# Attention and a gated feed-forward on one core: every bfloat16 product of TensorE given as two of 64 weight columns

## The chip, the core and the metric

The kernel runs on one core of a Trainium2 chip. A core has TensorE (matrix products; PE in the profile, with its weight loads as PEld), VectorE (DVE), ScalarE (ACT), GpSimd (POOL) and SyncE (SP, which here only issues transfers). Products are written to PSUM, which has eight banks; everything else lives in SBUF, and transfers to and from the chip's memory are run by 16 DMA engines. The metric is the device time of one execution in microseconds, less is better.

## The reference

For 8 batches of 8 heads with 576 positions of 64 values each, causal attention with a forgetting gate, and then a gated feed-forward layer on all 4,608 tokens:

```python
scores = scale * np.matmul(q, k.transpose(0, 1, 3, 2))
log_f = np.log(np.clip(f, 0.0001, 1.0))
cum = np.cumsum(log_f, axis=-1)
decay = cum[:, :, :, None] - cum[:, :, None, :]
scores = np.where(causal, -1000000000.0, scores + decay)
attn = softmax(scores)                       # max taken off, exp, divided by the sum
attn_out = np.matmul(attn, v)
x = attn_out.transpose(0, 2, 1, 3).reshape(B * S, H * D)      # 4608 x 512
g = x @ w_gate                                                # 512 x 1536
silu = g * (1.0 / (1.0 + np.exp(-g)))
out = (silu * (x @ w_val)) @ w_out                            # 1536 x 512
```

Inputs and the result are float32; the kernel computes its products in bfloat16 and sums them in float32.

## The kernel before

Two heads form a pair, `p`, of which there are 32, four in each batch. The 128 rows of a tile are 64 query rows of one head and the same 64 of the other. Each head's 576 positions are nine blocks of 64 (`i`), in two groups: `g` = 0 holds blocks 0 to 3 and `g` = 1 blocks 4 to 8.

On TensorE, a head pair goes through these steps:

- Transposes of q and k (L467; L546 for the first four pairs). The inputs lie with positions on the partitions; products with the identity turn them, six of 96 columns for k and eight of 72 for q. The result goes to PSUM (`tx`) and is copied to `kt` and `qz`. `qz` holds each head's query block in its own half of the partitions, with zeros in the other, so that one product of 128 rows serves both heads.
- Scores (L594) and mask (L598). For each block `i` the weights are `qz[:, i]`, 128 columns, and the moving operand is the pair's keys up to the block's end, 64 to 512 columns at a time. On the diagonal block a second product, of the identity with a mask of 64 columns, adds the causal mask. The table `BANKS` says which products share a PSUM bank (`sp`).
- VectorE adds the decay and takes the row minimum (L622), ScalarE takes the exponential (L642), GpSimd divides by the sum into `pk` (L678).
- The attention weights are transposed from `pk` to `pT`: for the first eight pairs on TensorE (L708, 128 columns each, 25 of them per pair), for the others by a DMA.
- Output (L734): for every chunk `c` of 128 key positions, two products, one for each head: 64 weight columns of `vt` and that head's columns of `pT`, written to PSUM partitions 0 to 63 and 64 to 127. So this product alone is already given as two halves of 64 weight columns. For `g` = 1 the five chunks have 320, 320, 320, 192 and 64 columns, for `g` = 0 the two chunks 256 and 128; from the ninth pair on the two groups are one operation of 14 products.
- `spread` copies the result to `xT` (L758), where it lies as the feed-forward needs it.

The feed-forward works on tiles of tokens, `TILES` = 256, 256, seven times 512, 256, 128, 128. `gate` (L816) multiplies `wg` and `wv`, as weights of 128 x 128, with `xT`, four products into each 128 rows of the hidden layer; tanh, two VectorE products and a rounding to bfloat16 follow (`th`, `hh`). `project` (L844) takes `hh` as weights and 512 columns of `wo` as the moving operand, twelve products for each 128 tokens, and the result goes out through `ot`.

The order of all instructions is set before launch: `Plan.order` is a list scheduler with a cost for each operation and engine, priorities, and the tiles' buffers; its result is written out as it stands. The costs given for TensorE's operations (`mm`, and the sums beside the transposes) are numbers in the source and do not follow from what is issued. Ahead of the first scores, `select` (L395) spreads the decay by a float32 product; it is not touched.

Of the kernel before, what the change touches and what calls it, by code (L numbers as in the profile page):

```python
# [32 lines left out]
class Plan:  # L33
# [29 lines left out]
    def order(self):  # L63
# [126 lines left out]
        assert len(done) == len(self.ops), [o.writes for o in self.ops if o.start is None][:10]  # L190
        self.span = max(o.end for o in done)
        return sorted(done, key=lambda o: (o.start, o.n))


def mm(*cols):
# [4 lines left out]
def kernel(  # L200
# [234 lines left out]
    def prepare(p):  # L435
        s = first[p]
        if p < NHALF:
            prepare_parts(p)
            return
        for name in ("k", "q"):  # L440
            fk, bk = (name + "f", p), (name + "b", p)
            KR, KC = ROWS[name]
            pl.key(bk, name + "b")

            def cast(e, name=name, fk=fk, bk=bk, KR=KR):
                src = pl.buf(fk)[0:KR, :, :].rearrange("p h (r d) -> p r h d", d=D)
                dst = pl.buf(bk)[0:KR, :, :, :]
                if e == "ACT":
                    nc.scalar.activation(dst, src, AF.Copy, scale=-scale if name == "q" else 1.0)
                elif name == "q":  # L450
                    eng[e].tensor_scalar(dst, src, -scale, 1.0, op0=ALU.mult, op1=ALU.mult)  # L451
                else:
                    eng[e].tensor_copy(dst, src)
            engs = {"POOL": 850 if p < 8 else 800 if name == "k" else 1010}
            if p < NPB:
                engs = {"POOL": 850, "ACT": 850, "DVE": 500} if name == "k" else {"POOL": 1050, "ACT": 1050, "DVE": 680}
            o = pl.op(engs, cast, [fk], [bk], s - 1 + (name == "q") * .1)
            o.bias = SPARE if p else {}
            tk = ("tt", name, p)
            pl.key(tk, "tx", line="q")  # L460
            ok = ("kt", p) if name == "k" else ("qz", p)
            pl.key(ok, ok[0])

            def transpose(e, bk=bk, tk=tk, KR=KR, KC=KC):
                src = pl.buf(bk).rearrange("p r h d -> p r (h d)")
                for j in range(KC):
                    nc.tensor.transpose(half(tk)[:, KR * j:KR * j + KR], src[0:KR, j, :], ident[0:KR, 0:KR])  # L467
            pl.op({"PE": KC * (KR / 2.4 + 2.5)}, transpose, [bk], [tk, ok], s - 1, lat=200)
            halves = [(0, P, None)] if name == "k" else [(0, 64, 0), (64, 128, 1)]
            for a, z, h in halves:  # L470
                def evac(e, a=a, z=z, h=h, tk=tk, ok=ok, KC=KC):
                    if h is None:
                        src = half(tk)[a:z, 0:S].rearrange("r (j p) -> r p j", j=KC)
                        dst = pl.buf(ok)[a:z, :].rearrange("r (p j) -> r p j", j=KC)
                    else:
                        src = half(tk)[a:z, 0:S].rearrange("r (j i p) -> r i p j", j=KC, i=NB)
                        dst = pl.buf(ok)[a:z, :, h, :].rearrange("r i (p j) -> r i p j", j=KC)
                    if e == "ACT":
                        nc.scalar.copy(dst, src)
                    else:  # L480
                        nc.vector.tensor_copy(dst, src)  # L481
                o = pl.op({"ACT": 600, "DVE": 680}, evac, [tk] + ([("z", "qz", p)] if h is not None and p < len(pl.pools["qz"]) else []), [ok, (ok, "done")], s - .9)
                o.bias = LATER if p >= 8 else {}
# [34 lines left out]
    def prepare_parts(p):  # L518
        for name, x, a, z, r, n in parts(p):
# [23 lines left out]
            def transpose(e, bk=bk, tk=tk, r=r, w=m * n):  # L543
                src = pl.buf(bk).rearrange("p r h d -> p r (h d)")
                for j in range(r):
                    nc.tensor.transpose(half(tk)[:, w * j:w * j + w], src[0:w, j, :], ident[0:w, 0:w])  # L546
            pl.op({"PE": r * (m * n / 2.4 + 2.5)}, transpose, [bk], [tk] + (oks if x == "A" else []), pr, lat=200, holds=oks)
            for u in range(n):
                for lo, hi, h in ([(0, P, None)] if name == "k" else [(0, 64, 0), (64, 128, 1)]):
# [31 lines left out]
    def scores(p, g):  # L581
# [3 lines left out]
        for n, bank in enumerate(BANKS[g]):  # L585
# [4 lines left out]
            def mult(e, bank=bank, sk=sk):  # L590
                sp, kt, qz, o = pl.buf(sk), pl.buf(("kt", p)), pl.buf(("qz", p)), 0
                for i, a, z in bank:
                    last = z == QB * (i + 1)
                    nc.tensor.matmul(sp[:, o:o + z - a], qz[:, i, :, :].rearrange("p h r -> p (h r)"), kt[:, a:z],  # L594
                                     start=True, stop=not last or p >= MFROM)
                    o += z - a
                    if last and p < MFROM:
                        nc.tensor.matmul(sp[:, o - QB:o], ident, mask, start=False, stop=True)  # L598
            cols = [z - a for _, a, z in bank] + [64 for i, a, z in bank if z == QB * (i + 1) and p < MFROM]
            pl.op({"PE": mm(*cols)}, mult, pair_done(p, g) + ["mask"], [sk], pr, lat=220, holds=[("kt", p), ("qz", p)])  # L600
            o = 0
# [46 lines left out]
    def normalize(p, g):  # L648
# [51 lines left out]
        for a in range(0, NSL[g], 8):  # L700
            z = min(a + 8, NSL[g])
            bk = ("tt", p, g, a)
            pl.key(bk, "gv", line="p")
            bank = lambda bk=bk: half(bk)

            def transpose(e, a=a, z=z, bank=bank):
                for x in range(a, z):
                    nc.tensor.transpose(bank()[:, P * (x - a):P * (x - a) + P], pl.buf(kk)[:, x, :], ident)  # L708
            pl.op({"PE": 56 * (z - a)}, transpose, [kk], [bk], s, lat=300)

            def evac(e, a=a, z=z, bank=bank):
                dst = pl.buf(tk)[:, a:z, :].rearrange("p s k -> p (s k)")
                (nc.scalar.copy if e == "ACT" else nc.vector.tensor_copy)(dst, bank()[:, :P * (z - a)])  # L713
            pl.op({"DVE": 64 * (z - a) / .96 + 90, "ACT": P * (z - a) * .833 + 110}, evac, [bk], [tk], s)
# [86 lines left out]
    def gate(t, tok, n):  # L801
        nf = 512 // n
        x0 = tok % NRING
        assert x0 + n <= NRING
        for u in range(KF // nf):
            fcs = range(u * nf, u * nf + nf)
            xs = [("x", hp, m) for hp in range(KD) for m in range(tok // QB, (tok + n) // QB)]
            pr = 1000 + t * 20 + u
            for nm, wt in (("wg", wg), ("wv", wv)):
                bk = (nm, t, u)  # L810
                pl.key(bk, "gv", line="f")

                def mult(e, wt=wt, bk=bk, fcs=fcs):
                    for j, fc in enumerate(fcs):
                        for ko in range(KD):
                            nc.tensor.matmul(pl.buf(bk)[:, j * n:j * n + n], wt[:, ko, fc * P:fc * P + P],  # L816
                                             xT[:, ko, x0:x0 + n], start=ko == 0, stop=ko == KD - 1)
                o = pl.op({"PE": mm(*[n] * (KD * nf))}, mult, xs + [(nm, fc) for fc in fcs], [bk], pr, lat=220)
                gates_of[t] = o
            pl.key(("th", t, u), "th")  # L820
            pl.key(("hh", t, u), "hh")
            pl.op({"ACT": 487}, lambda e, u=u: nc.scalar.activation(pl.buf(("th", t, u)), pl.buf(("wg", t, u)), AF.Tanh, scale=0.5),  # L822
                  [("wg", t, u)], [("th", t, u)], pr - 5000, lat=120)
            pl.op({"DVE": 605}, lambda e, u=u: nc.vector.scalar_tensor_tensor(  # L824
                pl.buf(("th", t, u)), pl.buf(("th", t, u)), 1.0, pl.buf(("wg", t, u)), op0=ALU.add, op1=ALU.mult),
                [("th", t, u), ("wg", t, u)], [("u", t, u)], pr - 5000, lat=180)
            pl.op({"DVE": 605}, lambda e, u=u: nc.vector.tensor_mul(pl.buf(("hh", t, u)), pl.buf(("th", t, u)), pl.buf(("wv", t, u))),  # L827
                  [("u", t, u), ("th", t, u), ("wv", t, u)], [("hh", t, u)], pr - 5000, lat=100)

    def project(t, tok, n):  # L830
        nf = 512 // n
        for ms in range(n // P):
# [4 lines left out]
            for a, z in ((0, DM // 2), (DM // 2, DM)) if end else ((0, DM),):  # L837
                bk = ("op", t, ms, a)
                pl.key(bk, "gv", line="o")
                for f0 in range(0, KF, 4):  # L840
                    def mult(e, f0=f0, ms=ms, bk=bk, a=a, z=z):
                        for fc in range(f0, f0 + 4):
                            hh = pl.buf(("hh", t, fc // nf))
                            nc.tensor.matmul(pl.buf(bk)[:, 0:z - a], hh[:, (fc % nf) * n + ms * P:(fc % nf) * n + ms * P + P], wo[:, fc, a:z],  # L844
                                             start=fc == 0, stop=fc == KF - 1)
                    pl.op({"PE": mm(*[z - a] * 4)}, mult, [("hh", t, fc // nf) for fc in range(f0, f0 + 4)] +
                          [("wo", fc) for fc in range(f0, f0 + 4)] + ([(bk, f0)] if f0 else []), [bk, (bk, f0 + 4)], pr, lat=220)

# [123 lines left out]
```

## Time and profile before

| what | value |
|---|---|
| median of 3 runs | 419.02 us (418.44 to 419.73) |
| profiled execution: span | 417.2 us |
| PE busy | 398.3 us, 95% |
| DVE / ACT / POOL busy | 79% / 74% / 60% |
| TensorE instructions in the program | 6,579 |

The page gives no time of the profiled execution other than its span, from the first to the last instruction; the median of the runs lies 1.8 us above it. In the profile, a row of the timeline gives the start in us, the time from the first start to the last end, the engine, the source line, the operation, the tiles, and the shape: `128*64` means 128 rows of the array and 64 weight columns, and `128x320` means 320 columns streamed. The end of a matmul is modelled and reaches into the next, so what a product costs in a stream is read from start to start. A table of stretches gives for each engine its busy us and, in brackets, the number of its instructions in the stretch.

### The profile page before, as it was taken

To read this page: it belongs to the slowest core of one execution; us is meant where nothing else is said; L and a number is where in the kernel's file an instruction comes from. 1 tells how busy PE (TensorE), PEld (TensorE's weight loads), DVE (VectorE), ACT (ScalarE), POOL (GpSimd) and SP (SyncE) were. 2 spreads that over 40 slices of the span, in tenths; PEclk is the share of its full clock that TensorE was granted. 3 is DMA by queue.
4 is the path that set the end of the run, shared out by engine and by line. 5 is a ranking of instruction groups with operands and counts; after the bars stand their busy time and mean duration, and the time that the engine had idled before them with its cause. 6 is when DMAs were issued, how large, how long until landed. Compare 5 with 4: busy or idle time off the path is not lost.

```text
span 417.2 us, 9955 instructions
## 1 busy us (share of the span) xinstructions
PE 398.3 (95%) x3250; PEld 232.3 (56%) x3296; DVE 328.9 (79%) x1065; ACT 310.3 (74%) x872; POOL 251.7 (60%) x459
## 2 busy tenths in 40 slices
PE   1979999999999999999999999999999999999996
PEld 0636878665555555555555554555555444457675
DVE  5688999999998899989897797798967764565232
ACT  4798999989995999899999984798996533232221
POOL 7589698987887897976968678267773400000000
PEclk9998999999999999999999999999999999999999
DMA  9999979695999999899999999848999211000211
GB/s 183 253 210 225 190 135 252 159 234 141 200 229 215 264 218 236 203 232 222 228 234 218 240 221 223 194 116 190 221 217 186 55 37 50 25 27 25 77 52 52
DMA packets 144004, 71.83 MB, mean 172 GB/s; under 512 B 117904, under 2 KB 131728, under 8 KB 143952
## 3 DMA queue, kind: packets, MB, share of 16 engines
q1 hardware_dynamic: 137568, 65.95, 71.1%
q0 software_dynamic: 5808, 4.72, 7.6%
q10 hardware_dynamic: 576, 0.52, 0.5%
q8 instruction: 26, 0.43, 0.4%
q14 instruction: 26, 0.21, 0.3%
HBM read 46.65 MB, written 9.58 MB: 135 GB/s over the span
## 4 chain that ended last, share of the span: by engine, by line
PE 86%; DVE 4%; issue 1%; ACT 0%
PE gv L816 43%; PE gv L844 22%; PE sp L594 9%; PE tx L734 6%; PE tx L467 3%; PE sp L598 2%; PE gv L708 2%; DVE t L622 1%; DVE pT L713 1%; DVE hh L827 1%; DVE th L824 1%; DVE qz L481 1%; DVE kt L481 0%; ACT ot L851 0%; DVE tm L622 0%
## 5 line engine op out<-in xcount | busy, mean ns | idle before, releaser
L622 DVE CUSTOM_DVE_ANT_0 t<-sp,cb 128x320 f32<-128x320 f32 (+7 forms) x288 | 130.4, 475 | 12.1 <-PE sp L598 8.6
L678 POOL TENSOR_SCALAR pk<-e,lr 128x128 bf16<-128x128 f32 (+3 forms) x190 | 100.5, 533 | 61.8 <-DVE lr L660 16.5
L816 PE MATMUL gv<-xT,wg 128*128 128x512 bf16 (+2 forms) x563 | 110.6, 327 | 0.8
L816 PE MATMUL gv<-xT,wv 128*128 128x512 bf16 (+2 forms) x562 | 109.3, 324 | 0.9
L844 PE MATMUL gv<-wo,hh 128*128 128x512 bf16 (+1 forms) x425 | 104.2, 373 | 0.8
L824 DVE SCALAR_TENSOR_TENSOR th<-th,gv 128x512 f32<-128x512 f32 x108 | 73.9, 684 | 39.3 <-ACT th L822 38.3
L822 ACT ACTIVATE th<-gv 128x512 f32<-128x512 f32 x108 | 64.1, 594 | 44.0 <-PE gv L816 43.1
L642 ACT ACTIVATE e<-t,tm 128x576 f32<-128x576 f32 (+4 forms) x160 | 88.7, 556 | 8.9 <-DVE tm L622 8.3
L827 DVE TENSOR_TENSOR hh<-th,gv 128x512 bf16<-128x512 f32 x108 | 73.7, 685 | 8.7 <-PE gv L816 4.9
L642 ACT ACTIVATE eo<-t,tm 128x128 f32<-128x128 f32 (+3 forms) x128 | 71.1, 556 | 4.7 <-DVE tm L622 2.9
L594 PE MATMUL sp<-kt,qz 128*128 128x448 bf16 (+6 forms) x320 | 71.9, 293 | 1.5 <-DVE tm L622 1.4
L678 POOL TENSOR_SCALAR pk<-eo,lr 128x128 bf16<-128x128 f32 (+3 forms) x127 | 67.6, 532 | 5.4 <-DVE lr L660 3.1
L816 PEld LDWEIGHTS <-wg 128*128 128x128 bf16 x576 | 49.8, 98 | 35.7
L816 PEld LDWEIGHTS <-wv 128*128 128x128 bf16 x576 | 48.9, 98 | 33.7 <-issue 0.3
L844 PEld LDWEIGHTS <-hh 128*128 128x128 bf16 x444 | 39.9, 98 | 39.0
L598 PE MATMUL sp<-mask,ident 128*128 128x64 bf16 x288 | 48.0, 197 | 0.0
L594 PEld LDWEIGHTS <-qz 128*128 128x128 bf16 x320 | 30.9, 100 | 20.9 <-DVE tm L622 0.9
L851 ACT ACTIVATE ot<-gv 128x512 f32<-128x512 f32 (+1 forms) x31 | 17.9, 580 | 27.1 <-PE gv L844 26.2
L598 PEld LDWEIGHTS <-ident 128*128 128x128 bf16 x288 | 27.2, 100 | 12.6 <-issue 1.9
L734 PE MATMUL tx<-pT,vt 128*64 128x320 bf16 (+4 forms) x448 | 29.6, 266 | 1.9 <-DVE pT L713 1.3
L451 POOL TENSOR_SCALAR qb<-qf 72x1024 bf16<-72x1024 f32 x28 | 29.1, 1041 | 3.1 <-DMA qf<-in_q_dram 2.0
L642 ACT ACTIVATION_READ_ACCUMULATOR e<-t,tm 128x1 f32 x160 | 30.6, 192 | 0.0
(69 smaller groups left out, 389.0 us busy)
## 6 DMA issues: line engine op xcount, KB each, us to landing
out_dram<-ot SPq DMA_DIRECT2D x35, 256.0 KB
vf<-in_v_dram SPq DMA_DIRECT2D x32, 256.0 KB
cb<-cum_f SPq DMA_DIRECT2D x56, 144.0 KB
kf<-in_k_dram SPq DMA_DIRECT2D x28, 288.0 KB
qf<-in_q_dram SPq DMA_DIRECT2D x28, 288.0 KB
wo<-in_moe_w_out_dram POOLq DMA_DIRECT2D x3, 512.0 KB, 10.8
vf<-in_v_dram SPq DMA_DIRECT2D x8, 128.0 KB
wv<-in_moe_w_val_dram POOLq DMA_DIRECT2D x2, 512.0 KB, 8.4
```

The costliest lines, as they stand in the source:

```text
L451: eng[e].tensor_scalar(dst, src, -scale, 1.0, op0=ALU.mult, op1=ALU.mult)
L594: nc.tensor.matmul(sp[:, o:o + z - a], qz[:, i, :, :].rearrange("p h r -> p (h r)"), kt[:, a:z], start=True, stop=not last or p >= MFROM)
L598: nc.tensor.matmul(sp[:, o - QB:o], ident, mask, start=False, stop=True)
L622: nc.vector.tensor_tensor_reduce(out=pl.buf(tk)[:, a:z], in0=pl.buf(sk)[:, o:o + z - a], in1=pl.buf(("cm", p))[:, i, :] if own else pl.buf ...
L642: nc.scalar.activation(pl.buf(ek)[:, :L], pl.buf(tk)[:, :L], AF.Exp, bias=pl.buf(("tm", p, g))[:, 0, i:i + 1], scale=-1.0, accum_out=pl.bu ...
L678: eng[e].tensor_scalar(dst, src, r, 1.0, op0=ALU.mult, op1=ALU.mult)
L734: nc.tensor.matmul(xo[r, 0:QB * n], vt[:, c, 2 * hp + h, :], pT[:, a:a + n, 64 * h:64 * h + 64], start=(c == 0), stop=(c == nch - 1))
L816: nc.tensor.matmul(pl.buf(bk)[:, j * n:j * n + n], wt[:, ko, fc * P:fc * P + P], xT[:, ko, x0:x0 + n], start=ko == 0, stop=ko == KD - 1)
L822: pl.op({"ACT": 487}, lambda e, u=u: nc.scalar.activation(pl.buf(("th", t, u)), pl.buf(("wg", t, u)), AF.Tanh, scale=0.5), [("wg", t, u)], ...
L824: pl.op({"DVE": 605}, lambda e, u=u: nc.vector.scalar_tensor_tensor(pl.buf(("th", t, u)), pl.buf(("th", t, u)), 1.0, pl.buf(("wg", t, u)), ...
L827: pl.op({"DVE": 605}, lambda e, u=u: nc.vector.tensor_mul(pl.buf(("hh", t, u)), pl.buf(("th", t, u)), pl.buf(("wv", t, u))), [("u", t, u), ...
L844: nc.tensor.matmul(pl.buf(bk)[:, 0:z - a], hh[:, (fc % nf) * n + ms * P:(fc % nf) * n + ms * P + P], wo[:, fc, a:z], start=fc == 0, stop=f ...
```

## The change

Two helpers are added. `columns` gives a product as two: the first uses weight columns 0 to 63 and writes partitions 0 to 63 of the output, the second uses columns 64 to 127 and writes partitions 64 to 127; both stream the same moving operand and carry the same start and stop marks. `turned` does so for transposes. Every bfloat16 product and transpose but L734 goes through them; L734 has this form already and L395 is float32. The planner's costs are as they were, and the order of operations is kept. Each of these products now takes two weight loads and two matmuls.

```diff
+def columns(nc, out, lhsT, rhs, **kw):
+    for h in range(2):
+        c = slice(64 * h, 64 * h + 64)
+        nc.tensor.matmul(out[c, :], lhsT[:, c], rhs, **kw)
+
+
+def turned(nc, out, src, ident):
+    for h in range(2):
+        c = slice(64 * h, 64 * h + 64)
+        nc.tensor.transpose(out[c, :], src[:, c], ident)
...
-                    nc.tensor.transpose(half(tk)[:, KR * j:KR * j + KR], src[0:KR, j, :], ident[0:KR, 0:KR])
+                    turned(nc, half(tk)[:, KR * j:KR * j + KR], src[0:KR, j, :], ident[0:KR, 0:KR])
...
-                    nc.tensor.transpose(half(tk)[:, w * j:w * j + w], src[0:w, j, :], ident[0:w, 0:w])
+                    turned(nc, half(tk)[:, w * j:w * j + w], src[0:w, j, :], ident[0:w, 0:w])
...
-                    nc.tensor.matmul(sp[:, o:o + z - a], qz[:, i, :, :].rearrange("p h r -> p (h r)"), kt[:, a:z],
-                                     start=True, stop=not last or p >= MFROM)
+                    columns(nc, sp[:, o:o + z - a], qz[:, i, :, :].rearrange("p h r -> p (h r)"), kt[:, a:z],
+                            start=True, stop=not last or p >= MFROM)
...
-                        nc.tensor.matmul(sp[:, o - QB:o], ident, mask, start=False, stop=True)
+                        columns(nc, sp[:, o - QB:o], ident, mask, start=False, stop=True)
...
-                    nc.tensor.transpose(bank()[:, P * (x - a):P * (x - a) + P], pl.buf(kk)[:, x, :], ident)
+                    turned(nc, bank()[:, P * (x - a):P * (x - a) + P], pl.buf(kk)[:, x, :], ident)
...
-                            nc.tensor.matmul(pl.buf(bk)[:, j * n:j * n + n], wt[:, ko, fc * P:fc * P + P],
-                                             xT[:, ko, x0:x0 + n], start=ko == 0, stop=ko == KD - 1)
+                            columns(nc, pl.buf(bk)[:, j * n:j * n + n], wt[:, ko, fc * P:fc * P + P],
+                                    xT[:, ko, x0:x0 + n], start=ko == 0, stop=ko == KD - 1)
...
-                            nc.tensor.matmul(pl.buf(bk)[:, 0:z - a], hh[:, (fc % nf) * n + ms * P:(fc % nf) * n + ms * P + P], wo[:, fc, a:z],
-                                             start=fc == 0, stop=fc == KF - 1)
+                            columns(nc, pl.buf(bk)[:, 0:z - a], hh[:, (fc % nf) * n + ms * P:(fc % nf) * n + ms * P + P], wo[:, fc, a:z],
+                                    start=fc == 0, stop=fc == KF - 1)
```

## The prediction

> **What bounds the kernel now.** I read the page's head and its chain of waits first, then TensorE's own waits, then the busy time of each engine stage by stage.
>
> ```profile
> span 417.2 us, 9955 instructions
> PE 398.3 (95%) x3250; PEld 232.3 (56%) x3296; DVE 328.9 (79%) x1065; ACT 310.3 (74%) x872; POOL 251.7 (60%) x459
> PE 86%; DVE 4%; issue 1%; ACT 0%
> q8 instruction: 26, 0.43, 0.4%
> ```
>
> ```profile
> PE tx L546 <- ACT kb L530: 6.9, 1, 6.9
> PE sp L594 <- DVE tm L622: 1.4, 4, 0.4
> ```
>
> The stages (columns: the stretch, its us; busy us and, in brackets, the number of instructions of PE, PEld, DVE, ACT and POOL; then granted clock, DMA share, GB/s):
>
> ```profile
> 0.00:36.00 36.00, 23.07 (x159) 14.32 (x160) 26.00 (x104) 26.00 (x79) 27.18 (x70) 0.96 1.05 216
> 36.00:60.00 24.00, 23.71 (x300) 19.64 (x299) 22.80 (x67) 22.34 (x57) 18.96 (x29) 0.99 0.87 174
> 60.00:84.00 24.00, 23.89 (x265) 18.12 (x265) 23.54 (x81) 23.29 (x65) 21.73 (x38) 1.00 0.93 204
> 84.00:150.00 66.00, 65.41 (x561) 36.46 (x570) 61.09 (x219) 58.50 (x175) 53.83 (x95) 1.00 0.99 215
> 150.00:250.00 100.00, 99.31 (x799) 53.26 (x810) 88.56 (x322) 93.82 (x278) 78.62 (x138) 1.00 1.08 225
> 250.00:338.00 88.00, 87.37 (x631) 44.68 (x643) 71.23 (x224) 63.48 (x182) 51.37 (x94) 1.00 0.80 171
> 338.00:391.00 53.00, 52.69 (x295) 28.62 (x296) 27.42 (x40) 15.68 (x28) 0.00 (x0) 1.00 0.08 31
> ```
>
> TensorE carries 86% of the chain, and from 36 us to the end its waits for others are a few microseconds. Whatever lengthens or shortens the stream of products there moves the end one for one. The clock is full from 36 us on. The runs' median, 419.0 us, lies 1.8 us above this execution's span; I add that to every span below.
>
> **What a product of two halves costs on the array.** The kernel already has such pairs: the attention output (L734) gives each 64 weight columns to one half of the array. Here is one such group between full-width products.
>
> ```profile
> 336.83 0.59 PE L816 MATMUL gv<-xT,wg 128*128 128x512 bf16 x2
> 337.35 0.88 PE L734 MATMUL tx<-pT,vt 128*64 128x320 bf16 x14
> 338.01 0.22 PE L734 MATMUL tx<-pT,vt 128*64 128x128 bf16 x2
> 338.16 0.39 PE L816 MATMUL gv<-xT,wv 128*128 128x512 bf16 x1
> 337.78 0.23 PEld L734 LDWEIGHTS <-vt 128*64 128x64 bf16 x6
> ```
>
> And a stretch of the early stage, with full-width products alone of every size (columns: start, us from first start to last end, count):
>
> ```profile
> 42.35 0.62 PE L708 MATMUL gv<-ident,pk 128*128 128x128 bf16 x8
> 42.80 0.19 PE L594 MATMUL sp<-kt,qz 128*128 128x64 bf16 x1
> 42.83 0.19 PE L598 MATMUL sp<-mask,ident 128*128 128x64 bf16 x1
> ...
> 43.77 0.42 PE L467 MATMUL tx<-ident,kb 96*128 96x96 bf16 x6
> 44.03 1.04 PE L816 MATMUL gv<-xT,wv 128*128 128x256 bf16 x8
> 44.91 0.33 PE L708 MATMUL gv<-ident,pk 128*128 128x128 bf16 x3
> 45.07 0.42 PE L467 MATMUL tx<-ident,qb 72*128 72x72 bf16 x8
> 45.33 0.33 PE L594 MATMUL sp<-kt,qz 128*128 128x384 bf16 x1
> ...
> 45.69 1.04 PE L816 MATMUL gv<-xT,wg 128*128 128x256 bf16 x8
> 46.66 0.71 PE L734 MATMUL tx<-pT,vt 128*64 128x320 bf16 x10
> ```
>
> Start to start, a full-width product takes 0.45/8 = 56 ns at 128 columns, 0.88/8 = 110 at 256, 0.26/6 = 43 at 96, 0.26/8 = 32 at 72 and 30 at 64 (42.80 to 42.83): about 0.42 ns a column. The L734 group streams 320, 320, 320, 192, 64, 256 and 128 columns, each twice. Its first six pairs, 2 x 1472 columns, took 337.35 to 338.01, 0.66 us; one after the other they would need 2944 x 0.42 = 1.24 us. So the two halves run side by side, and a pair costs what one full-width product costs. The change therefore adds no array time by these rows; I take 0 (ends: 0, and a doubling if two streams of the same operand, which L734 never has, could not run together).
>
> **What goes.** Turning the array from full width to halves and back costs time: the eight 256-column products from 45.69 need 0.88 us, yet L734 starts 0.97 later, 0.09 us lost; on the way back 128 columns need 0.056, yet 0.15 passes from 338.01 to 338.16, 0.09 to 0.10 lost. Afterwards nearly everything is in halves and nothing turns. There are 448 L734 products, in groups of 14 (10 and 4 for the first eight head pairs): 40 groups, of which 36 lie after 36 us. 36 x 0.19 = 6.8 us gone, all on the path; the first four stand before waits and count as 0. [...]
>
> **What is added: instructions.** Each of the bfloat16 products other than L734 becomes two loads and two products where there was one of each; the program of TensorE grows from 6,579 to 12,255 instructions. Other engines keep their order and tiles, and an evacuation waits for the second half, which starts a few ns after the first: 0. Code is fetched twice as often, 0.4% of the DMA engines' time becoming 0.8%; I take 0 (it is 1 us for some 250 instructions).
>
> What the trace hardly shows is how fast TensorE's sequencer hands instructions over, since it is ahead almost always:
>
> ```profile
> L967 PEldq DRAIN x2: 13/1190/2368, 411.6 to 416.7; - x2
> 411.61 2.06 PEld L844 LDWEIGHTS <-hh 128*128 128x128 bf16 x17
> 9.71 0.28 PEld L395 LDWEIGHTS gv<-t,one 64*128 64x128 f32 x1 [2.43 <-issue]
> 9.74 0.76 PE L395 MATMUL gv<-t,one 64*128 64x256 f32 x1 [2.20 <-DVE t L373]
> 11.39 0.28 PEld L395 LDWEIGHTS gv<-t,one 64*128 64x128 f32 x1 [0.20 <-issue]
> 11.39 0.79 PE L395 MATMUL gv<-t,one 64*128 64x256 f32 x1
> 392.84 5.36 PE gv L816 x96
> ```
>
> It reached the closing drain at 411.6 with 17 loads and their products still to start: a head start of at least 34 instructions. Only once did it stand with an empty queue, at a semaphore before L395 at 9.6 us. There the product came 0.03 us after its load, where the same pair, when queued (11.39), starts together. That is the one sight of the hand-over: 30 ns an instruction. From above, 192 instructions ran in 5.36 us without a stall, so 192f < 5.36 + 34f, f < 34 ns. From below, 0. I take 30, the one direct row; it is a single one, and for another type.
>
> At 30 ns a pair needs 4 x 30 = 120 ns, more than every product of up to 256 columns. Instructions after are 2 x (PE + PEld) of a stretch, less L734's own, which stay (same columns, L734 alone, then clock and DMA):
>
> ```profile
> 36.00:60.00 24.00, 3.03 (x40) 1.97 (x40) 0.99 0.87 174
> 60.00:84.00 24.00, 2.13 (x28) 1.24 (x28) 1.00 0.93 204
> 84.00:150.00 66.00, 5.45 (x84) 3.59 (x84) 1.00 0.99 215
> 150.00:250.00 100.00, 8.77 (x140) 5.95 (x140) 1.00 1.08 225
> 250.00:338.00 88.00, 8.55 (x138) 5.93 (x140) 1.00 0.80 171
> ```
>
> - 36 to 60 us: 2 x 599 - 80 = 1118, 33.5 us against 24: +9.5.
> - 60 to 84: 2 x 530 - 56 = 1004, 30.1 against 24: +6.1.
> - 84 to 338: 2094, 2938 and 2270, so 62.8, 88.1 and 68.1 us against 66, 100 and 88: it fits on average. The bursts: six transposes of 96 columns take 0.26 us and their 24 instructions 0.72; eight of 72, 0.26 and 0.96. Each misses 0.46 or 0.70 us, and the head start is 34 x 0.03 = 1.0 us, refilled by the 512-column products beside them (0.216 us against 0.120). I take 0, and the turns there, 26 groups x 0.19, give 4.9 back.
> - 338 to 391: 35 against 53: 0.
> - The last two tiles have 128 tokens: twice 96 products at 56 ns, 384 instructions, 11.5 us against 5.36, less the head start of 1.0: 2 x 5.1 = +10.3.
> - 0 to 36: 2 x 319, less some 50 of L734 and L395: 588, 17.6 us, among waits; bursts +2 (0 to 5).
>
> Sum: 9.5 + 6.1 + 10.3 + 2 - 4.9 = +23. 417.2 + 23 + 1.8 = **442 us**. By 33 ns the same sum is 12.9 + 9.1 + 3.1 + 12.4 + 4 - 3 = +38.5, 457.5 us.
>
> [...]
>
> **The rivals.**
> - *The hand-over is quick, and the turns that vanish decide: faster.* For it: the waits above name no stall of TensorE's own making, and a queued load and product start together. Against: the 30 ns row. Below 15 ns even the 128-token tiles keep up (5.36/350), and the time is 417.2 - 6.8 + 1.8 = 412 us (to 415, where VectorE, busy 23.5 of 24 us from 60 to 84, and ScalarE, 94 of 100 from 150, do not follow). The point of decision is about 22 ns: there 36 to 84 us just keeps up (24/1118 = 21.5 ns), the tail loses 2 x (384 x 0.022 - 0.75 - 5.36) = 4.7, bursts some 2, and the 6.8 are used up: 419.
> - *In between, 22 to 28 ns.* Nothing excludes it: 419 to 436 us.
> - *Loads of halves bind.* [...] The row at 337.78 is against it: three pairs of half-width loads in 0.23 us, so a pair takes 0.08 at most. Were each pair bound to that, the tail would lose 192 x 0.024 = 4.6 us, and each of the 32 head pairs 14 x 0.044 on its transposes and 11 x 0.05 on its score and mask products of 64 columns, 1.2 us, 37 in all: 417 + 42 - 7 + 2 = 454 us.
> - *The change does not pair up:* with one operand streamed to both halves, the halves run in turn. No row speaks for it; the time would be near twice 398 busy us.
>
> **How the numbers follow.** Chances: hand-over at 28 ns or more 0.47 (436 to 460, likeliest 442), in between 0.13 (mostly slower, a third of it within or under the bound), quick 0.36 (410 to 418), loads 0.02 (454), no pairing 0.02. No change means within 0.3%, 1.3 us, about what these runs can tell apart. Range 410 to 458: it must hold both signs; the likeliest case's own is 434 to 458. Faster 0.36, same 0.04, slower 0.60.
>
> **What would show it.** Right: in the 128-token tiles a pair starts about 120 ns after the one before, the 96 products last some 10.5 us instead of 5.36, the stretch 338 to 391 keeps its length, L734 starts and ends with no 0.09 us gap. Wrong: those tiles keep 56 ns a pair; then the hand-over is quick and the time falls by the turns. Pairs whose halves start a full product apart, or narrow products at 80 ns a pair and no slower at 256 columns, would mean the last two.

## The result and the profile after

The changed kernel takes 421.6 us (median of 9 runs, 421.09 to 424.29) against 419.23 for the kernel before (9 runs beside them): a ratio of 1.0064, 95% interval 1.0043 to 1.0086, so 1.8 to 3.6 us slower. I forecast slower, but by 23 us. The profiled execution took 423.35 us, 1.75 above its median, with a span of 421.6 us; it is 4.4 us longer than the span shown of before, and the accounts below explain those 4.4.

The page's head, the first line of its chain, and the queue that fetches code:

```profile
span 421.6 us, 15689 instructions
PE 397.3 (94%) x6134; PEld 299.1 (71%) x6134; DVE 329.2 (78%) x1065; ACT 311.3 (74%) x872; POOL 252.3 (60%) x459
PE 58%; DMA 14%; ACT 6%; POOL 5%; DVE 4%; issue 3%; SPq 2%; POOLq 0%; DVEq 0%; ACTq 0%
q8 instruction: 48, 0.79, 0.8%
```

TensorE has nearly twice the products and is busy for no longer. What has changed is the chain: TensorE fell from 86% to 58%, and transfers, which were not in it, hold 14%. Some of its longest pieces (start, us, what):

```profile
247.95 7.48 DMA pT<-pk
255.70 7.45 DMA pT<-pk
...
265.05 9.77 DMA pT<-pk
...
342.63 75.70 PE gv L198 x1100
```

The stages, in the same columns as before:

```profile
36.00:60.00 24.00, 22.97 (x558) 21.59 (x553) 23.53 (x71) 22.21 (x57) 19.78 (x31) 1.00 0.91 192
60.00:84.00 24.00, 22.41 (x478) 20.21 (x474) 22.14 (x76) 21.96 (x60) 20.47 (x35) 1.00 0.88 185
84.00:150.00 66.00, 65.46 (x1064) 43.84 (x1060) 61.43 (x221) 58.20 (x175) 52.75 (x93) 1.00 1.00 207
150.00:250.00 100.00, 98.35 (x1468) 67.21 (x1466) 87.24 (x315) 93.04 (x276) 78.52 (x139) 1.00 1.07 222
250.00:338.00 88.00, 85.55 (x1142) 60.88 (x1140) 70.39 (x229) 65.12 (x187) 54.16 (x98) 1.00 0.91 182
338.00:391.00 53.00, 53.00 (x597) 45.76 (x595) 30.36 (x45) 16.76 (x29) 0.00 (x0) 1.00 0.12 35
```

From 36 to 84 us TensorE stands for 2.6 us where it stood for 0.4, and from 150 to 338 for 4.1 where it stood for 1.3. The last stretch shown is full in both, to 0.3 us.

**The hand-over.** This row, from the first 128-token tile, is the one that the forecast turned on (PE, start and us, count):

```profile
396.98 1.07 PE L198 MATMUL gv<-xT,wg 128*64 128x128 bf16 x31
397.87 0.22 PE L198 MATMUL gv<-xT,wv 128*64 128x128 bf16 x1
```

31 halves start in 0.89 us, 29 ns each and 57 ns a pair, what a full-width product of 128 columns took (56). Each half is a load and a product, so TensorE takes 62 instructions in 0.89 us, 14 ns each, and no sign of a limit is seen at that pace. The 75.70 us at the end of the chain hold 1,100 halves without one wait.

**The halves and the turns.** Around an L734 group in the changed kernel:

```profile
340.92 1.09 PE L198 MATMUL gv<-xT,wg 128*64 128x512 bf16 x8
341.78 0.86 PE L746 MATMUL tx<-pT,vt 128*64 128x320 bf16 x13
342.47 0.38 PE L198 MATMUL gv<-xT,wv 128*64 128x512 bf16 x1
342.48 0.22 PE L746 MATMUL tx<-pT,vt 128*64 128x128 bf16 x1
342.53 1.03 PE L198 MATMUL gv<-xT,wv 128*64 128x512 bf16 x7
```

Eight halves of 512 columns take 0.86 us, four times 0.215: a pair costs one full-width product. The group (L746 now) starts with no gap before it. The next product starts 0.06 us after the group's last pair of 128 columns began, which is what such a pair costs; before it was 0.15. So the array does what the forecast said, and both turns are gone.

**Where the time came from.** TensorE's waits:

```profile
PE gv L204 <- issue: 1.6, 3, 0.7
PE tx L746 <- DMA pT<-pk: 1.4, 2, 0.9
...
PE tx L204 <- POOL qb L463: 0.9, 2, 0.5
PE gv L198 <- DVE th L836: 0.8, 1, 0.8
PE tx L204 <- issue: 0.7, 1, 0.7
```

Two kinds are new. The first, "issue", has no releaser at all. One of them, in loads (upper two rows) and products (lower two):

```profile
49.19 0.21 PEld L204 LDWEIGHTS <-pk 128*64 128x64 bf16 x3
50.22 0.42 PEld L204 LDWEIGHTS <-pk 128*64 128x64 bf16 x13 [0.83 <-issue]
```

```profile
49.31 0.22 PE L204 MATMUL gv<-ident,pk 128*64 128x128 bf16 x1
50.22 0.58 PE L204 MATMUL gv<-ident,pk 128*64 128x128 bf16 x13 [0.69 <-issue]
```

The transposes stop in the middle of one operation, whose data are all there. There are five such stops, at 43.75, 50.22, 67.44, 73.64 and 80.38 us, of 0.31, 0.91, 0.74, 0.86 and 0.62 us from start to start, about 3.2 us beyond the normal distance; before has none. Counted along TensorE's program all five stand at the same place modulo 256 instructions (from one stop to the next 128 loads and 128 products, between 50.22 and 67.44 us 384 and 384); 48 fetches of 0.79 MB are 16 KB each, and 12,255 instructions over 48 fetches are 255 each, so 256 instructions are one fetched block. In the trace the block for the stop at 50.22 left at 47.50 and landed at 48.82, and TensorE went on 1.40 us later; the other four land 1.3 to 1.5 us before it goes on as well. The packet before each of these left only 3.0 to 4.2 us after the block ahead of it had been entered; where no stop follows, between 50 and 61 us, it left after 1.5 to 1.9. So from the entry into one block to the first instruction of the next, up to about 4.2 + 1.2 + 1.4 = 6.8 us pass (why the packet leaves later before a stop, no row shows), and in halves TensorE uses one up in 5.1 to 5.4 us at this stage (50.22 to 55.30 and 55.30 to 60.66); before it took 9.8 to 10.6. Before, with the longer time for each block, the arrival stayed hidden; in halves it does not, at a DMA share of 0.91 and 0.88 in these two stretches, where before had 0.87 and 0.93.

The second kind is waits for data that come by transfer: `pT` directly, `kb` and `qb` through GpSimd's casts, and what hangs on them. Setting each product against the same product of before shows where the two kernels part: the change is 0.6 us ahead at 37 us, 1.9 behind at 80, 1.2 behind at 115, 2.3 at 155, 5.8 at 274 to 286, 4.3 at 342, and 4.3 at every later point. From 37 us on it lost 4.9 us net. The 36 groups gave 6.8, so 11.7 us of stops and waits are new: 3.2 for code, and about 8.5, the remainder, for the rest, most of it between 140 and 275 us. In the profile's list these waits look shorter, since the modelled end of a product reaches into the wait behind it.

### The profile page after: what moved, and what is told of

It reads as the page before. It is cut to its first block, busy times and chain, and to the rows that moved or that the text cites. A ratio compares the mean times of both kernels' runs of the same rounds, so it can differ in the third digit from the quotient of the medians.

```text
span 421.6 us, 15689 instructions
## 1 busy us (share of the span) xinstructions
PE 397.3 (94%) x6134; PEld 299.1 (71%) x6134; DVE 329.2 (78%) x1065; ACT 311.3 (74%) x872; POOL 252.3 (60%) x459
## 4 chain that ended last, share of the span: by engine, by line
PE 58%; DMA 14%; ACT 6%; POOL 5%; DVE 4%; issue 3%; SPq 2%; POOLq 0%; DVEq 0%; ACTq 0%
PE gv L198 45%; DMA pT<-pk 6%; PE sp L198 6%; DMA qf<-in_q_dram 4%; POOL pk L690 4%; PE tx L746 3%; ACT e L654 2%; PE gv L204 2%; PE tx L204 2%; DVE t L634 2%; DMA cb<-cum_f 1%; ACT eo L654 1%; DMA vf<-in_v_dram 1%; SPq L442 1%; ACT th L834 1%
## 5 line engine op out<-in xcount | busy, mean ns | idle before, releaser
L198 PE MATMUL gv<-xT,wg 128*64 128x512 bf16 (+2 forms) x1152 | 115.5, 326 | 0.8 <-DVE th L836 0.8
L198 PE MATMUL gv<-xT,wv 128*64 128x512 bf16 (+2 forms) x1152 | 115.6, 326 | 0.0
L198 PE MATMUL gv<-wo,hh 128*64 128x512 bf16 (+1 forms) x888 | 110.5, 374 | 0.0
L198 PEld LDWEIGHTS <-wg 128*64 128x64 bf16 x1152 | 66.4, 110 | 21.0 <-issue 1.1
L198 PEld LDWEIGHTS <-wv 128*64 128x64 bf16 x1152 | 65.4, 110 | 19.3 <-issue 0.3
L198 PE MATMUL sp<-kt,qz 128*64 128x512 bf16 (+7 forms) x640 | 76.6, 293 | 2.2 <-DVE tm L634 1.3
L198 PEld LDWEIGHTS <-hh 128*64 128x64 bf16 x888 | 60.3, 110 | 19.8
L198 PEld LDWEIGHTS <-qz 128*64 128x64 bf16 x640 | 43.3, 112 | 16.7 <-issue 4.1
L198 PE MATMUL sp<-mask,ident 128*64 128x64 bf16 x576 | 53.0, 196 | 0.0
L198 PEld LDWEIGHTS <-ident 128*64 128x64 bf16 x576 | 36.0, 113 | 7.0
L746 PE MATMUL tx<-pT,vt 128*64 128x320 bf16 (+4 forms) x448 | 30.5, 264 | 3.0 <-DMA pT<-pk 1.4
L746 PEld LDWEIGHTS <-vt 128*64 128x64 bf16 x448 | 25.6, 111 | 9.2 <-issue 3.2
## 6 DMA issues: line engine op xcount, KB each, us to landing
wo<-in_moe_w_out_dram POOLq DMA_DIRECT2D x3, 512.0 KB, 10.6
```

Of the source, the lines that this page charges most:

```text
L198: nc.tensor.matmul(out[c, :], lhsT[:, c], rhs, **kw)
L746: nc.tensor.matmul(xo[r, 0:QB * n], vt[:, c, 2 * hp + h, :], pT[:, a:a + n, 64 * h:64 * h + 64], start=(c == 0), stop=(c == nch - 1))
```

## The experiments

Theories after the result. HAND-OVER: my own, the sequencer hands instructions over too slowly. CODE: the doubled program costs, by stops and by slowing other transfers. STREAMS, later HALVES: two streams in the array disturb the memories or the transfers. PACE, formed after the first runs: the transfers were a second bound close behind TensorE, so that a TensorE freed of its turns runs into them. In all of them the order of the operations is that of before; a flag set by the planned start of an operation (some 5 us behind the trace) says which are given in halves.

**Halves only at the end.**

```diff
+            HALVES[0] = o.start >= 277000
             o.fn(o.eng)
```

> Products are given as halves only from the 26th head pair on (the last seven output groups, all remaining feed-forward tiles, the 128-token tiles among them); before that everything is at full width. The output is the reference's. Three theories stand. CODE: halves cost nothing on the array, each output group that no longer turns the array saves 0.19 us, and what is lost comes from the doubled code: TensorE waits for a block of code where instructions are dense (43 to 81 us), and the fetches slow the transfers where these are saturated (100 to 280 us). Here neither stage has halves: 7 x 0.19 less one turn of 0.09, 1.2 us faster than before, a ratio near 0.997. HAND-OVER (the prediction's): 30 ns an instruction, so the two 128-token tiles lose 10 us: ratio 1.02. STREAMS: two halves that read the same operand slow the transfers; nothing is saturated this late, so also about 1.2 us faster.

Measured: 418.1 us against 419.63, ratio 0.996 (0.9937 to 0.9982). This is faster than both kernels, and it is the version to keep. The table further down has it gaining 1.2 us from 291 to 337 us, for the turns of six L734 groups at 0.19 (1.1), and nothing behind that. The 128-token tiles, which I had costed at 10.3 us, cost nothing: HAND-OVER is refuted.

**Full width, doubled code.**

```diff
-                        for ko in range(KD):
-                            nc.tensor.matmul(pl.buf(bk)[:, j * n:j * n + n], ...
+                        for c in range(0, n, 128):
+                            for ko in range(KD):
+                                nc.tensor.matmul(pl.buf(bk)[:, j * n + c:j * n + c + 128], ...
```

and the score products of 128 columns or more cut in two.

> Everything at full width as before, but the code is made as long as with halves in another way: each gate product is given in pieces of 128 columns streamed, each score product of 128 columns or more in two pieces. The program of TensorE holds 11,699 instructions (before 6,579, halves 12,255); the turns of the array stay. The output is the reference's. By the spacing of 56 ns at 128 columns and 216 at 512 this costs the array 672 x 7 ns on the gates of 512 tokens, 288 x 3 on those of 256 and about 0.5 us on the scores, 6 us in all. CODE: stalls of TensorE at block boundaries without any semaphore between 40 and 85 us, 1 to 3 us in sum, and between 100 and 266 us SyncE's queue spends 145 to 152 us on its transfers (before 141.5, halves 152.6); total 8 to 13 us slower than before. STREAMS (halves themselves slow the transfers): no such stalls beyond the array's 6 us, SyncE's queue at 141 to 143 us; total 6 us slower.

Measured: 426.62 us, ratio 1.0177 (1.014 to 1.0214), 7.0 us more, between the two expectations, with no stop for code. The pieces themselves cost some 6 us, so TensorE became slower together with the doubling of its code, and a block lasted it 7.2 us or more from 38 to 105 us. It doesn't decide; it needed a partner with the same work on TensorE, which a later run has.

**Fewer transfers.** The loads of v are left out for all but the first batch, in the kernel before and in the changed one:

```diff
-lambda e, c=c, n=n, fk=fk: nc.sync.dma_start(
+lambda e, c=c, n=n, fk=fk: None if b else nc.sync.dma_start(
```

> The kernel before without the loads of v for the second to the eighth batch: its casts read what the first batch left, so that part of the result is left out; all other work is as it was. 35 of 40 loads of v are gone, so the transfers are lighter. TensorE bounds the kernel before, so all theories expect 0 to 1.5 us less than before: 417.5 to 419.

> The changed kernel, without the same loads of v (the same part of the result left out). CODE and STREAMS: with transfers that keep up, the waits for them from 140 to 280 us, some 7 us, go, and the vanished turns show: 2 to 6 us faster than the lighter kernel before, the stalls at code blocks between 43 and 81 us staying in part. HAND-OVER or any loss inside TensorE: as much slower than the lighter kernel before as the changed kernel is than its own, 2 to 4 us slower.

Measured: the kernel before is unmoved, 419.67 us, ratio 1.0 (0.9979 to 1.0021). The changed one takes 416.33, 0.9924 (0.9896 to 0.9953): with the queue relieved the same change is 3.3 us *faster*. So the loss hangs on the transfers, and about half of the 6.8 us for the turns comes out once they let it. The stretch from 80 to 280 us shows it best, first in the changed kernel and then in the same without the loads of v (columns as in the stages):

```profile
80.00:280.00 200.00, 194.98 (x2954) 131.33 (x2956) 174.57 (x611) 173.91 (x504) 148.35 (x258) 1.00 1.01 208
80.00:280.00 200.00, 199.85 (x3028) 135.59 (x3024) 180.32 (x636) 179.01 (x528) 155.70 (x275) 1.00 0.87 186
```

With the DMA share at 0.87 instead of 1.01, TensorE has no wait over 0.15 us there, although the code is as long and VectorE and ScalarE do more. From 87 to 337 us this kernel gains 4.0 us on the kernel before, of the 4.9 that its 26 groups can give. So neither the halves, nor the doubled code, nor VectorE and ScalarE hold TensorE up there by themselves; it took the full transfers, with their DMA share of 1.01. Whether SyncE's queue binds there or the 16 DMA engines behind it, no run separates: leaving out loads relieves both. One stop for code is left, and its share of the waits is small:

```profile
PE gv L198 <- DMA wg<-in_moe_w_gate_dram: 0.8, 1, 0.8
PE gv L204 <- issue: 0.5, 1, 0.5
```

**Which stage.** Halves from about 80 us on, and the complement:

```diff
+            HALVES[0] = o.start >= 75000      # the complement: o.start < 75000
```

> Halves from about 80 us on, full width before; the output is the reference's. The dense stage that showed stalls at code blocks is at full width again. If the stalls of 43 to 81 us and the lateness that they hand on were the whole loss: 29 output groups x 0.19 = 5.5 us faster than before. If the doubled code, or the halves, also slow the saturated transfers from 100 to 280 us, as the lighter pair of kernels suggests: no stall without a semaphore before 85 us, but waits for q, k and transposed weights of 3 to 7 us between 140 and 280 us, and a time within 2.5 us of before on either side.

> Halves until about 80 us only, full width after; the output is the reference's. CODE: the stalls at code blocks between 43 and 81 us come back, 2 to 3.5 us, seven output groups no longer turn (7 x 0.19 = 1.3), from 100 us on everything is as before: 0.5 to 2.5 us slower than before. If stalls there were hidden by waits that come anyway: 1 us faster than before.

Measured: from 80 us on 422.3, ratio 1.0053 (1.0024 to 1.0083); until 80 us 420.72, 1.0031 (1.0004 to 1.0058), both against 420.06. The waits part cleanly by kind. Until 80 us, where three stops of 1.7, 1.2 and 1.7 us stand at block ends:

```profile
PE gv L213 <- issue: 2.5, 2, 1.5
...
PE tx L213 <- issue: 1.5, 1, 1.5
```

From 80 us on, no stop for code before 85 us, and transfers:

```profile
PE tx L755 <- DMA pT<-pk: 2.7, 4, 1.0
...
PE tx L213 <- POOL kb L474: 2.0, 1, 2.0
```

**The price of a turn.** Halves only for the `wg` products from 338 to 391 us, where no transfer matters: 19 groups, 38 turns that weren't there.

```diff
+            HALVES[0] = 333000 <= o.start < 386000 and o.writes[0][0] == "wg"
```

> The price of a turn by itself: the kernel before, with the wg gate products alone in halves between 338 and 391 us, where the transfers are idle and TensorE alone sets the time. 19 groups of wg products then stand between full-width ones, 38 turns of the array and 200 instructions more; the output is the reference's. If a turn costs 0.095 us wherever it stands: 19 x 0.19 = 3.6 us slower than before, ratio 1.0086. If the 0.09 us belong to the output product's own weights or its place: no slower.

Measured: 423.47, ratio 1.0088 (1.0069 to 1.0107) where 1.0086 was expected: 3.7 us for 38 turns, 0.097 each (0.08 to 0.12 by the interval). In its trace the products of this stretch fall back by 4.3 us, 0.11 each.

**Halves from 245.**

```diff
+            HALVES[0] = o.start >= 245000
```

> As the kernel with halves from the 26th head pair on, but from about 250 us, so that three more output groups no longer turn, while the last saturated 25 us of transfers get the doubled code. The output is the reference's. Turns alone: 0.6 us faster than that kernel, 1.8 faster than before. If the doubled code costs the transfers more than that: as fast as before or slower.

Measured: 417.96, ratio 0.9965 (0.9936 to 0.9994). It can't be told from the run from the 26th head pair on; the groups that it frees between 250 and 280 us are lost in two new waits, 0.3 us idle for `kb` at 261 and 1.1 for `pT` at 269.

**Pace, code and halves in the saturated stage.** Three kernels side by side, with nearly the same work for TensorE from 80 to 280 us. One leaves out 23 gate products, one gives its gate products in pieces of 128 columns and leaves out 38, and one has halves in that stretch alone and leaves out nothing (its turns go instead).

```diff
 # 23 left out
-                        for ko in range(KD):
+                        kd = KD - LESS[0]
+                        for ko in range(kd):
...
+            LESS[0] = o.eng == "PE" and 75000 <= o.start < 277000 and w[0] == "wg" and TILES[w[1]] == 512 and w[2] % 2 == 0 and taken < 23
+            taken += LESS[0]
 # pieces, 38 left out
+                        w = P if SPLIT[0] else n
+                        for c in range(0, n, w):
...
+            SPLIT[0] = o.eng == "PE" and 75000 <= o.start < 277000 and w[0] in ("wg", "wv") and TILES[w[1]] == 512
+            LESS[0] = SPLIT[0] and w[2] % 2 == 0 and taken < 38
 # halves in the window
+            HALVES[0] = 75000 <= o.start < 277000
```

> Full-width products as in the kernel before, but 23 of the 512-column gate products of the stretch from about 80 to 280 us are left out (one of four in 23 groups), so that TensorE has 23 x 0.216 = 5.0 us less to do there, about what halves save there on turns (26 groups x 0.19 = 4.9). Code and shapes are the same. PACE (the transfers of SyncE's queue are at their limit there, so a TensorE that goes faster runs into them): most of the 5.0 us is lost again in waits for kb, qb and pT; between 2 us faster and no change. CODE or HALVES (the transfers are slowed by what the change itself brings): 4 to 5 us faster, ratio 0.988 to 0.991, with no new wait of over 0.5 us.

> Full width, but the gate products of 512 columns of the same stretch are given in four pieces of 128 columns (444 products become 1776 at 56 ns), and 38 of the 444 are left out, so that TensorE's work is that of the run with 23 left out (406 x 0.224 = 91.0 us, 421 x 0.216 = 90.9). It has 2,406 TensorE instructions more than that run, some nine more blocks of code to fetch in the stretch, and no halves. CODE: 3 to 6 us slower than the run with 23 left out, with waits for transfers or stops without a releaser. PACE and HALVES: within 1 us of it.

> Halves only in the stretch from about 80 to 280 us, full width before and after. The turns that go there save 4.9 us, and the code of the stretch doubles. PACE: within 1.5 us of the run with 23 products left out. CODE: within 1.5 us of the run with pieces, and well above the run with 23 left out. HALVES (two streams at once disturb the rest, whatever the code): 2 us or more slower than both. From the runs with halves from 80 us on (2.2 us above the kernel before) and from the 26th head pair on (1.5 below) I expect 3 to 5 us above the kernel before.

| TensorE from 80 to 280 us | median us | ratio to before (419.47) | 95% interval |
|---|---|---|---|
| 5.0 us less work, same code | 418.57 | 0.998 | 0.9951 to 1.0009 |
| the same, code in pieces, full width | 424.1 | 1.0118 | 1.0066 to 1.017 |
| halves, turns gone | 422.67 | 1.0086 | 1.0054 to 1.0119 |

The stretch before, and with 23 products left out:

```profile
80.00:280.00 200.00, 198.40 (x1596) 106.94 (x1624) 177.89 (x626) 176.77 (x519) 153.06 (x270) 1.00 0.99 212
80.00:280.00 200.00, 195.69 (x1574) 104.79 (x1603) 177.92 (x627) 177.05 (x519) 153.78 (x270) 1.00 0.99 212
```

Of 5.0 us of work taken from TensorE, which is busy for 198.4 of these 200 us before, 0.9 comes out at the end, and no gain at all lies within the interval. TensorE's idle time grows instead, from 1.6 to 4.3 us. The longest waits are for `qb`, whose loads come by SyncE's queue, 1.2 us; shorter ones, 0.2 to 0.3 us each, are for VectorE and ScalarE. That is PACE, and it would have cost the forecast's "quick" case most of its gain with no halves anywhere. With the same work and more code the time is 5.5 us longer (1.0118/0.998 = 1.014, about 1.008 to 1.020 with both intervals). That is what CODE expected; but the pieces also load their weights four times as often, and these runs do not part the two. The halves are no worse than the pieces, 1.4 us better at the medians with overlapping intervals: HALVES as a cause of its own isn't needed.

The mechanism in rows: SyncE's queue issued its transfers one after the other, and from 101 to 266 us there was little time between them: in the kernel before the issues fill 139.6 of 162.6 us. The same three groups of issues with 23 products left out, and then with pieces (start, us that the issues hold the queue):

```profile
149.67 4.52 SPq L694 DMA_TRANSPOSE pT<-pk  x1
154.25 2.63 SPq L777 DMA_DIRECT2D vf<-in_v_dram  x3
156.92 1.31 SPq L426 DMA_DIRECT2D kf<-in_k_dram  x1
```

```profile
150.38 7.56 SPq L695 DMA_TRANSPOSE pT<-pk  x1
157.99 4.21 SPq L778 DMA_DIRECT2D vf<-in_v_dram  x3
162.24 1.22 SPq L427 DMA_DIRECT2D kf<-in_k_dram  x1
```

They start 0.7 us apart; the load of k goes out 5.3 us later, and TensorE stands for its transposes:

```profile
169.11 0.43 PE L471 MATMUL tx<-ident,kb 96*128 96x96 bf16 x6 [2.93 <-POOL kb L457]
```

This one wait makes most of the pieces' loss in the traced execution: their distance to the kernel before goes from -0.02 to +4.30 us between 164 and 171 us, 2.93 of them idle and some 1.7 by a lower clock right behind it (last section).

From the first to the seventeenth `pT` transfer (114 issues, the same in all of these), the queue needs the following, worked out from its rows; "fetches" are blocks of code that arrive in the stretch.

| | stretch us | issues summed us | fetches |
|---|---|---|---|
| before | 162.6 | 139.6 | 10 |
| halves at the end / until 80 / `wg` late / from 245 | 164.8 / 163.9 / 164.1 / 165.6 | 142.9 / 147.8 / 144.1 / 146.2 | 10 |
| 23 products left out | 164.5 | 148.1 | 10 |
| full width, doubled code (slower TensorE) | 166.5 | 147.9 | 20 |
| pieces, 38 left out | 168.8 | 153.5 | 18 |
| the change | 168.7 | 152.6 | 18 |
| halves in the window / from 80 | 168.9 / 172.5 | 155.5 / 158.6 | 19 |

Six kernels with ten fetches need 162.6 to 165.6 us; the five with 18 to 20 need 166.5 to 172.5. A TensorE that goes 5 us faster does not shorten the stretch, and the longer code lengthens it by some 4 us. The sum of the issues doesn't part them as well: 139.6 to 148.1 us with ten fetches, 147.9 to 158.6 with 18 to 20. Without the loads of v, 94 issues are left and the stretch does follow TensorE: 161.9 us with ten fetches at full width, 159.9 with 18 in halves. The full-width run with doubled code shows the other side: its TensorE reaches the end of this stage about 3 us later by its own work, and so waits little.

How much later each kernel starts the same load of L734 than the kernel before (us, worked out from the traces; single executions, which differ by up to 1.6 us already in the first 36 us):

| at (us, before) | change | halves late | 23 left out | pieces | halves in window |
|---|---|---|---|---|---|
| 83.4 | +1.75 | -1.30 | -0.02 | +0.37 | -0.35 |
| 126.8 | +0.84 | -1.30 | -0.76 | -0.39 | -1.31 |
| 170.9 | +2.32 | -0.74 | -0.84 | +4.30 | +0.52 |
| 214.9 | +2.60 | -0.74 | -0.93 | +3.72 | +0.09 |
| 269.0 | +4.58 | -0.74 | -0.37 | +4.21 | +1.34 |
| 290.9 | +5.52 | -0.90 | -0.37 | +4.49 | +2.54 |
| 337.3 | +4.22 | -2.10 | -0.37 | +4.48 | +2.54 |

The three kernels of this table with longer code in this stage lose between 127 and 291 us; the one with less work alone gains 0.8 and gives half of it back. What stays open is the step between: whether it is the fetches that slow the transfers, and what they take from them. A `pT` issue that a fetch overlaps takes 5.4 us on average against 5.1 without one (187 issues in eleven traces), which is 3 us for eight more fetches, but an overlap is likelier for a longer issue. The pieces also load weights more often, as the halves do, and no run doubled the code without that, so the weight loads stand beside the fetches as a rival.

## Why the prediction was wrong

- **"Whatever lengthens or shortens the stream of products there moves the end one for one."** True behind 338 us (38 turns, 3.7 us) and from 291 to 337 us. This step failed from 80 to 280 us: 5.0 us less work moved the end by 0.9. TensorE was busy in 198.4 of 200 us there, but SyncE's queue, which issued one transfer at a time, was issuing for 139.6 of 162.6 us, and I quoted the DMA shares of 0.99 and 1.08 in those very rows without reading a bound in them. With lighter transfers TensorE kept 4.0 of the 4.9 us there. That TensorE was full showed what slower costs, one for one; it did not show that faster gains.
- **A pair costs what one full-width product costs, 0 added.** Right, for every size looked at: 0.215 us for 512 columns, 57 ns for 128, and nothing lost in the tail.
- **What goes: 0.19 us for each of 36 groups, 6.8 us.** Right in size (0.097 a turn measured against 0.09 to 0.10), and the light pair of runs shows half of it coming out at the end. In the changed kernel itself it was all given back.
- **"Code is fetched twice as often ... I take 0."** This step failed. It named the load on the DMA engines (0.4% to 0.8%) and not the latency: up to 6.8 us from one block to the next where TensorE stopped, against the 5.1 to 5.4 in which it used one up. Five stops cost 3.2 us in the profiled execution, and halves until 80 us alone cost 1.3 us net at the medians (1.0031, 1.0004 to 1.0058). In the saturated stage the run with 2,406 more instructions took 5.5 us more at equal work; that the fetches do it, and not the weight loads that came with them, is not shown. I named no cover for this zero; it was the 10 us that a block lasted, and the slack in SyncE's queue.
- **The hand-over, 30 ns, one direct row.** This step failed and brought the whole of the size: +9.5, +6.1, +10.3 and +2 in the sum are 0 as a hand-over. Measured is 14 ns an instruction or less. The row at 9.71 showed a load and its product, of another type, released by a semaphore; I took the 0.03 us between them, at a restart from a wait, for the pace of a stream, and no row showed that they are. The bound that I worked out from 192 instructions, below 34 ns, was true but too wide to help.
- **The sign and the stages it named.** That slower came out is luck: the hand-over on which it rested costs nothing, and what did cost stood in the sum as 0. From 36 to 84 us the kernel did get slower, as forecast, but by 3.2 us of stops where 15.6 were costed, and the cause is the block's arrival. Where queues were light, behind 338 us at a DMA share of 0.12 to 0.19, blocks were used up in 4.9 to 6.2 us in the last tiles without a stop. The tails, costed at +10.3, cost 0.
- **The rivals.** Quick hand-over was the right case for the sequencer, and its 412 us were wrong by the transfers: I allowed 3 us for VectorE and ScalarE not following and none for SyncE's queue. Loads of halves that bind, and halves that don't pair, are out: 57 ns a pair of 128 columns.

Summed by stage, from the runs that have one stage each: until 80 us +1.3, window +3.6, end -1.7, together +3.2 us against the measured 2.7 (0.64% of 419.2). Within the window: -4.9 by the turns, +4.1 since the transfers don't follow (5.0 less 0.9), and +5.5 by the larger code as the pieces show it, which makes 4.7 where 3.6 was measured. It closes to about 1 us; the fall of the clock in the pieces' trace, some 1.7 us, has no counterpart in the trace of the halves in the window.

## What to carry to other kernels

Before costing a change that speeds up a nearly full engine, look for the second bound: here, beside a queue that was issuing for 139.6 of 162.6 us in the same stage, 0.9 of 5.0 us arrived, and leaving out a few products is a cheap run that tells it. Before doubling an engine's instructions, compare how long it takes over a block of code, here 256 of TensorE's, with the time that a block needs to come beside the kernel's other transfers, here up to 6.8 us, and 7.3 from entry to entry in the run with halves until 80 us. Use the form that saves turns only where neither bound is near: the same halves from 280 us on, with the rest at full width, gave 1.5 us (0.996, 0.9937 to 0.9982).

## What the runs showed of the hardware

- TensorE took 14 ns an instruction over a whole tile of alternating loads and products, with 64-column loads 29 ns apart (the changed kernel, from 396.98 us).
- Two 64-column halves that stream the same operand ran side by side, as the two different operands of L734 do: 0.215 us a pair of 512 columns.
- A change between full width and halves cost 0.097 us, averaged over 38 (0.08 to 0.12).
- The clock fell after a short stop. With halves from 80 us on TensorE stood idle for 1.96 us before 130.17 us (a row of products, then two stretches with the columns of the stages, whose third number from the end is the granted clock):

```profile
130.17 0.45 PE L213 MATMUL tx<-ident,kb 96*64 96x96 bf16 x12 [1.96 <-POOL kb L474]
```

```profile
130.10:134.00 3.90, 3.83 (x32) 1.93 (x34) 1.10 (x3) 2.51 (x7) 2.19 (x4) 0.56 1.10 201
134.00:138.00 4.00, 4.00 (x82) 2.85 (x80) 3.61 (x14) 2.49 (x11) 2.30 (x4) 1.00 0.94 228
```

At 0.56 over 3.9 us, 3.9 x 0.44 = 1.7 us are lost on top of the wait. The run with pieces shows it once more behind its idle 2.93 us: 0.64 from 169 to 173 us and 0.94 from 173 to 177, again 1.7 us lost. Behind the stops for code of the run with halves until 80 us, up to 1.5 us idle, the clock stayed at 1.00. Of two such waits, 1.5 and 2.0 us, the longer thus cost nearly twice its size.
